# Sigmoid attention and a SwiGLU block on one core: exchanged PSUM tiles, visits one product later, a split transfer, two sums moved

## The chip, the cores and the metric

The kernel runs on one core of one Trainium2 chip. The metric is the time of the program on the device, in microseconds. Before the change it is 401.79 us, the median of three runs (401.12 to 402.68). The profiled execution took 401.11 us, of which its page shows a span of 399.1 us.

## The reference

```python
# q, k, v: (8, 12, 448, 64); 8 batches, 12 heads, 448 positions
scores = (q @ k.transpose(0, 1, 3, 2)) / sqrt(64) - log(448)
attn   = 1 / (1 + exp(-scores))             # sigmoid, no softmax over the row
x      = (attn @ v).transpose(0, 2, 1, 3).reshape(3584, 768)
g      = x @ w_gate                         # (768, 1536)
val    = x @ w_val                          # (768, 1536)
out    = (g * sigmoid(g) * val) @ w_out     # (1536, 768)
```

Since the sigmoid needs no sum over a row, every chunk of scores can be finished by itself. The inputs are float32; the kernel computes scores in bf16 and the rest in float16 with float32 sums.

## The kernel before

**Tiling.** The heads of a batch are taken in three groups of four, called quads here; quad n belongs to batch n // 3, so there are 24. The keys of a quad are cut into C = 7 chunks of 64 positions. One chunk of scores for four heads is four products of 64x64 tiles that fill both banks of one PSUM tile (`qk_tile`, L246-261). One ScalarE instruction makes the sigmoid of both banks (`sig_tile`, L273), or two, one for each bank, where the tile is wanted back early (L270). When seven chunks of a quad are through, `pv` (L276-314) multiplies them with V in 28 products and copies the two banks to two tiles xT on VectorE (L304 and L312). If `flip(n)` holds, the scores of the second pair of heads are written to the other half of the partitions, V is loaded by two transfers of 112 KB with heads in that order (L195), and the second xT tile is filled by one copy of 128 partitions. Otherwise V is one transfer of 224 KB (L197) and that copy is two of 64 partitions.

**The FFN.** Batches go in pairs pb = 0 to 3. `ffn1(b, f)` makes one block of 128 hidden features of one batch: six products for the gate and six for the value (L324), a sigmoid on ScalarE (L347), and two VectorE instructions (L349, L353) that leave the block hT. For the last two pairs most blocks are made two at a time by `double` (L434-507), which uses seven half-size products in place of eight, with sums of inputs made ahead; it is called the fast pair below. The output product of a pair is made likewise, in `ffn2_group` (L595), from sums of hT that `make_sums` (L533) computes on VectorE (L554). A group g is a generator that goes through seven products, in the order 1, 2, 6, 5, 7, 3, 4, with a snapshot or an addition out of PSUM after each (L644 on ScalarE, L646 and L651 on VectorE). `ffn2_part(pb, moves)` says which group steps next: (0, 1, 0, 1) does two products each of groups 0 and 1, and (0,) * 5 the rest of group 0.

**PSUM.** All of it is a ring of four tiles of two banks. `Banked` hands them out in turn, and a tile that an output group holds is left out (`kept`). When a group ends, the turn is set behind its tile. A product that writes a tile waits until the last reader of that tile is done.

**The order of work** on TensorE is the order in which the program is written out; nothing reorders it at run time. A planner in Python (L947-968) lists the FFN units with durations it assumes, and puts a visit to the attention in between when its due time has passed: a visit is four chunks (0 to 3) or three (4 to 6) of a quad. `attn_step` (L785-793) carries it out: two score tiles, then `pv` of the quad before if it is complete, then the other one or two. A condition in L953 keeps visits from some places, for instance right after a part of an output stage that mixes two groups. `budget` says how many of the pending sums VectorE makes after a unit, and the sums left over are made later.

**Other queues.** GpSimd casts q and k to bf16 (L204), issues the loads of V and of the weights, and makes some sums of its own, among them those of the rows left over at the end of each batch (`rest_sums`, L593). After each three-chunk visit of quad n it waits for the last sigmoid (`behind_visit`, L855), casts quad n+2 and issues its V; SyncE then transposes the casts by DMA (L211), loads q and k of quad n+4 (L183), and stores outputs (L565). Each queue goes in order.

Of the kernel before, what the change touches and what calls it, by code (L numbers as in the profile page):

```python
# [20 lines left out]
def kernel(  # L21
# [17 lines left out]
    NJ = H // 4  # L39
    NP = H // 2  # L40
    NF = DFF // 128
    NQ = B * NJ
    W2 = 2 * S
    LAST = B // 2 - 1
# [29 lines left out]
    ring_at = [0]  # L74
    ring_user = [None] * 4
    kept = set()
# [107 lines left out]
        qkv_st[(n, which)] = st  # L184

    def flip(n):
        return n > 5

    def load_v(n):
        t = v16p.tile([128, 2, S], FP16, tag="v16", name=f"v16_{n}")  # L190
# [55 lines left out]
    def qk_tile(n, c, at=None):  # L246
        sd = Banked(at=at)
        sc = sd.t
        qt, kt = qT[(n, 0)], qT[(n, 1, c)]
        for w in range(2):  # L250
            for h2 in range(2):
                r = slice(h2 * 64, h2 * 64 + 64)
                g = (w ^ (h2 and flip(n))) * 64
                nc.tensor.matmul(  # L254
                    out=sc[g:g + 64, h2, :S],
                    lhsT=kt[r, w * 64:(w + 1) * 64],
                    rhs=qt[r, :, w * 64:(w + 1) * 64],
                    start=True,
                    stop=True,
                )  # L260
        return sd
# [54 lines left out]
    V, G = nc.vector, nc.gpsimd  # L316
# [59 lines left out]
    def fast_w(i, kind):  # L376

        s, lo, hi = gcut[i]
        cs = slice(lo * 128, hi * 128)
        b11, b21 = wg16[s][:, 0::2, cs], wg16[s][:, 1::2, cs]  # L380
        b12, b22 = wv16[s][:, 0::2, cs], wv16[s][:, 1::2, cs]
        n = JT * (hi - lo) * 128
        at = {3: 0, 2: 1, 4: 2}.get(kind)
        if kind == 1:
            t = b12
        else:
            if i == 0:
                t = half_of(stg_a)[:, at * n:(at + 1) * n]
            elif i == 1 and kind == 3:
                t = half_of(ramp_a)[:, 8 * FW * hw:8 * FW * hw + n]  # L390
            elif i == 1:
                t = pt_f[:, (at - 1) * n:at * n]
            elif i == 2:
                t = pt_f[:, (at + 2) * n:(at + 3) * n]
            elif i == 3:
                o = JT * FW * 128 * 5 + NF * 128
                t = pt_f[:, o + at * n:o + (at + 1) * n]
            else:
                t = osp.tile([128, DM], FP32, tag="osb", name=f"g{kind}").bitcast(FP16)[:, :n]
            t = t.rearrange("p (j n) -> p j n", j=JT)  # L400
        gT[(i, kind)] = t
        a, b, op = {
            3: (b22, b12, SUB), 1: (b12, b11, SUB), 2: (b22, gT.get((i, 1)), SUB), 4: (b21, gT.get((i, 2)), SUB),
        }[kind]
        V.tensor_tensor(out=t, in0=a, in1=b, op=op)
# [118 lines left out]
    budget = {}  # L524
# [42 lines left out]
    def rest_h(pb, i):  # L567
        if pb == LAST:
            a, at = pt_f, 5 * JT * FW * 128
        else:  # L570
            a, at = half_of(ramp_a), 8 * FW * hw
        return a[:, at + i * 128:at + (i + 1) * 128]

    def rest_s(pb, kind, i):
        if pb == LAST:
            at = ((kind - 1) * HF + i) * 128
            return half_of(stg_a)[:, at:at + 128]
        return hS[(pb, kind, i)][:, :128]

    def keep_rest(pb, fs, copy):  # L580
        for f in fs:
            copy(out=rest_h(pb, f), in_=hT[(pb - 1, f)].rearrange("p b s -> p (b s)")[:, (C - 1) * 128:])

    def rest_sums(pb, eng):
        of = lambda f: hT[(pb, f)].rearrange("p b s -> p (b s)")[:, (C - 1) * 128:]
        for kind in (1, 2, 3, 4):
            for i in range(HF):
                f = 2 * i
                a, b, op = {
                    1: (of(f), of(f + 1), ADD), 2: (rest_s(pb, 1, i), rest_h(pb, f), SUB),  # L590
                    3: (rest_h(pb, f), of(f), SUB), 4: (rest_h(pb, f + 1), rest_s(pb, 2, i), SUB),
                }[kind]
                yield eng.tensor_tensor(out=rest_s(pb, kind, i), in0=a, in1=b, op=op)  # L593
# [124 lines left out]
    for pb in range(B // 2):  # L718
        for b in (2 * pb, 2 * pb + 1):
            f1_start[b] = tt  # L720
            for f in range(NF):
                if f not in FAST.get(pb, ()):
                    if b or f > 2:
                        units.append((FU1, ffn1, (b, f)))
                    tt += FU1
            f1_end[b] = tt
        for f in FAST.get(pb, ())[::2]:
            extra = {
                (LAST - 1, 0): ((0, 4), (1, 2)), (LAST - 1, 2): ((1, 4), (2, 3)),
                (LAST - 1, 4): ((2, 1), (2, 2)), (LAST - 1, 6): ((2, 4), (3, 3), (3, 1), (3, 2)),  # L730
                (LAST - 1, 8): ((3, 4),),
                (LAST, 0): ((4, 3),), (LAST, 2): ((4, 1),), (LAST, 4): ((4, 2),), (LAST, 6): ((4, 4),),
            }.get((pb, f), ())
            units.append((FU4, double, (pb, (f, f + 1), [lambda a=a: fast_w(*a) for a in extra])))
            tt += FU4
        skip = lambda: None
        w = lambda *a: lambda: [w_sum(*b) for b in a]
        o_units = [(0.0, make_sums, (99,))]
        part = lambda moves, *a: o_units.append((FU3 * len(moves) / 7, ffn2_part, (pb, moves) + a))
        if pb == 0:  # L740
            fill[(1, 7)] = [lambda: w_sum(0, 3), lambda: w_sum(0, 2)]
            fill[(1, 9)] = [lambda: w_sum(0, 1)]
            o_units += [(0.0, w_sum, a) for a in ((1, 3), (1, 2))]
            part((0, 1, 0, 1), ("1654", "154"), (skip, skip, w((1, 1))))
            part((0,) * 5, "", (w((0, 4), (1, 4)),))
            copies = [lambda f=f: keep_rest(1, (f, f + 1, f + 2), V.tensor_copy) for f in range(0, NF, 3)]
            part((1,) * 5, "", copies)
            part((2,) * 7, "654")
        elif pb == 1:
            part((0, 1, 0, 1), "1")  # L750
            part((0,) * 5)
            part((1,) * 5, "", (lambda: list(rest_sums(1, G)),))
            part((2,) * 3)
            part((2,) * 4)
            part((3,) * 3, "", (skip, lambda: fast_w(1, 3), lambda: fast_w(1, 1)))
            part((3,) * 4)
            o_units.append((0.0, sums_of_x, (LAST - 1,)))
        else:
            part((0, 1) * 7, "1", (skip, lambda: keep_rest(LAST, range(NF), nc.scalar.copy)) if pb < LAST else ())
            if pb == LAST:  # L760
                part((3,) * 7)
            part((2,) * 7)
        units += o_units
        tt += sum(u[0] for u in o_units)


    FIRST = f1_end[0] - 5.0
    PACE = ((2 * NJ, FIRST + 3.5), (3 * NJ - 1, FIRST + 28.9), (3 * NJ - 0.5, f1_end[1] - 0.1), (3 * NJ, FIRST + 40.5), (3 * NJ + 2, FIRST + 55.6), (6 * NJ + 1, f1_end[B - 5] - 1.0), (6 * NJ + 1.5, f1_end[B - 5]), (NQ, f1_end[B - 5] + 1.0))
    tiles = [(n, c) for n in range(NJ, NQ) for c in range(C)]
    visits = [tiles[:2], tiles[2:4]]  # L770
# [3 lines left out]
    vtime = []  # L774
    for grp in visits:
        n, c = grp[0]
# [3 lines left out]
        else:  # L780
            at = n + (0.5 if c else 0.0)
# [3 lines left out]
    def attn_step(group, pvs):  # L785
        late = 1 if pvs else 0
        for part in (group[:2], group[2:]):
            scs = [(n, c, qk_tile(n, c)) for n, c in part]
            while pvs:
                pv(pvs.pop(0))  # L790
            for i, (n, c, sc) in enumerate(scs):

                sig_tile(n, c, sc, split=len(group) == 4 and part[0] == group[0] and i == late)
# [12 lines left out]
    for i in range(8):  # L806
# [8 lines left out]
    copies = [  # L815
        trans_part(Dq, 0, 0, 0, 0, QS, V, dq[:, :QS]),
        trans_part(Dq, 1, 0, 0, QS, C, V, dq[:, QS:]),
    ]
# [130 lines left out]
    tcur = 3 * FU1  # L949
    since, was_v = 99.0, 9  # L950
    was, was_args = ffn1, (0, 2)
    for dur, fn, args in units:
        if visits and tcur >= vtime[0] and not (was is ffn2_part and len(set(was_args[1])) > 1) and not (was is ffn1 and was_args[0] < 2 and was_args[1] == 0) and (vtime[0] < FIRST + 4 or since > (3.8 if len(visits[0]) > 3 and visits[0][0][0] < 4 * NJ else 2.0)):  # L953
            seq.append((None, visits.pop(0), 0 if fn is ffn1 else 1))
            vtime.pop(0)
            since, was_v = 0.0, 0
        seq.append((fn, args, not visits and was_v == 1))
        was, was_args = fn, args
        was_v += dur > 0.0
        since += dur  # L960
        tcur += dur

    for i, (fn, args, _) in enumerate(seq):
        if fn is ffn1:
            ahead = [len(a) if f is None else 0 for f, a, _ in seq[i + 1:i + 3]] + [0, 0]
            budget[args] = 0 if args == (3, NF - 1) else 3 if ahead[0] else 0 if ahead[1] == 4 else 2
        if fn is double:
            args[2].append(lambda: make_sums(5))

# [70 lines left out]
```

## Time and profile before

| | before |
|---|---|
| Time, median of three | 401.79 us |
| TensorE busy | 388.6 us, 97% of the span |
| VectorE busy | 251.4 us, 63% |
| ScalarE busy | 237.3 us, 59% |
| GpSimd busy | 123.3 us, 31% |
| First FFN products | about 22 us after the start |
| First output stage (pair 0) | 98.1 to 124 us |
| Second output stage (pair 1) | 207.5 to 244 us |
| First fast pair | from 259.1 us |

The page names an instruction by its line in the kernel, its engine, and the tiles it writes and reads. In the timeline a line gives the start, the time from the first to the last of the instructions merged in it, and in brackets how long the engine had been idle before it and what ended that. A matmul's time there (0.35 us for 448 columns) is that of one instruction from end to end; since they overlap, the pace is read from one start to the next.

### The profile page before, as it was taken

The page shows a single profiled execution, that of the slowest core. Times are in us where ns is not written, and L with a number is a line of the kernel's source. Part 1 is how long each engine was busy: PE and PEld are TensorE (multiplying, and loading weights), DVE is VectorE, ACT ScalarE, POOL GpSimd, SP SyncE. Part 2 cuts the span into 40 slices and gives each one's busy share as a digit, 9 for nine tenths or more (in the row PEclk, how much of TensorE's full clock was granted, in tenths as well). Part 3 has the DMA queues.
Part 4 walks back from the last instruction along what each step waited for, and adds up shares of the span by engine and source line. Part 5 has one row for each costly group of instructions (what it writes and reads, how often), then busy time and mean ns, then how long its engine had stood idle before and what let it go on. Part 6 is the DMA issues. An engine that isn't in the chain of part 4 may idle for free.

```text
span 399.1 us, 8113 instructions
## 1 busy us (share of the span) xinstructions
PE 388.6 (97%) x3110; PEld 201.9 (51%) x3110; DVE 251.4 (63%) x505; ACT 237.3 (59%) x385; POOL 123.3 (31%) x203
## 2 busy tenths in 40 slices
PE   7799999999999999999999999999999999999995
PEld 3444544445555444444455555455555655555653
DVE  2637646688643444466674564699986558787553
ACT  5966785746456797779773467966653055656000
POOL 4538041421311353343330958600007400000900
PEclk9999999999999999999999999999999999999999
DMA  8999979996599777797778878000000520000055
GB/s 273 246 246 256 241 166 261 183 169 98 143 279 232 173 163 163 163 186 163 163 164 192 198 161 201 3 2 1 1 2 0 159 79 2 2 2 0 2 169 147
DMA packets 65574, 54.39 MB, mean 136 GB/s; under 512 B 36032, under 2 KB 61728, under 8 KB 65536
## 3 DMA queue, kind: packets, MB, share of 16 engines
q1 hardware_dynamic: 49264, 37.04, 35.1%
q0 software_dynamic: 15360, 15.34, 24.3%
q10 hardware_dynamic: 912, 1.51, 1.2%
q8 instruction: 24, 0.39, 0.4%
q14 instruction: 14, 0.11, 0.1%
HBM read 47.19 MB, written 11.01 MB: 146 GB/s over the span
## 4 chain that ended last, share of the span: by engine, by line
PE 93%; DMA 3%; DVE 1%; ACT 1%; issue 0%; SPq 0%; POOL 0%; DVEq 0%; ACTq 0%
PE ps_D L324 31%; PE ps_D L633 24%; PE ps_D L460 22%; PE ps_D L254 8%; PE ps_D L289 8%; DMA v<-in_v_dram 2%; DMA st<-in_q_dram 1%; DVE xT L312 1%; PE ps_D L223 0%; DVE xT L304 0%; ACT osb L644 0%; DVE T L229 0%; ACT small L490 0%; DVE osb L646 0%; DVE stg_a L646 0%
## 5 line engine op out<-in xcount | busy, mean ns | idle before, releaser
L273 ACT ACTIVATE pt_a<-ps_D 128x896 f16<-128x896 f32 x148 | 127.1, 920 | 41.5 <-PE ps_D L254 39.8
L324 PE MATMUL ps_D<-xT,wg 128*128 128x448 f16 x312 | 69.2, 353 | 0.2
L324 PE MATMUL ps_D<-xT,wv 128*128 128x448 f16 x312 | 68.5, 353 | 0.0
L349 DVE TENSOR_TENSOR t<-ps_D,s 128x448 f16<-128x448 f32 x52 | 32.4, 624 | 54.8 <-ACT s L347 54.2
L470 ACT ACTIVATE snap<-ps_D 128x448 f32<-128x448 f32 x66 | 34.2, 542 | 29.4 <-PE ps_D L460 27.5
L254 PE MATMUL ps_D<-T,T 64*64 64x448 bf16 x644 | 44.6, 358 | 2.2 <-DVE T L229 1.2
L324 PEld LDWEIGHTS <-wg 128*128 128x128 f16 x312 | 27.8, 98 | 34.0 <-issue 12.1
L324 PEld LDWEIGHTS <-wv 128*128 128x128 f16 x312 | 30.4, 98 | 28.9 <-issue 0.6
L347 ACT ACTIVATE s<-ps_D 128x448 f16<-128x448 f32 x52 | 28.7, 551 | 22.8 <-PE ps_D L324 22.8
L204 POOL CAST c<-stg_a 128x896 bf16<-128x896 f32 x40 | 36.5, 939 | 14.5 <-DMA stg_a<-in_q_dram 10.3
L633 PEld LDWEIGHTS <-S 128*128 128x128 f16 x312 | 30.2, 98 | 20.9 <-issue 1.3
L633 PE MATMUL ps_D<-ramp_a,S 128*128 128x384 f16 x234 | 40.2, 326 | 0.0
L289 PE MATMUL ps_D<-pt_a,v 64*64 64x448 f16 x672 | 36.0, 350 | 0.5 <-DMA v<-in_v_dram 0.5
L353 DVE SCALAR_TENSOR_TENSOR hT<-ps_D,t 128x448 f16<-128x448 f32 x52 | 32.5, 625 | 5.4
L651 DVE SCALAR_TENSOR_TENSOR osb<-ps_D,osb 128x384 f32<-128x384 f32 x40 | 22.3, 557 | 19.0 <-PE ps_D L633 16.7
L855 POOL CAST held<-S 128x1 bf16<-128x1 f16 x3 | 0.6, 190 | 107.7 <-ACT osb L644 55.7
L646 DVE TENSOR_SCALAR osb<-ps_D 128x384 f32<-128x384 f32 x37 | 20.6, 557 | 18.1 <-PE ps_D L633 15.1
L633 PEld LDWEIGHTS <-hT 128*128 128x128 f16 x228 | 22.1, 98 | 15.6 <-issue 1.3
L855 POOL CAST held<-pt_a 128x1 bf16<-128x1 f16 x13 | 2.5, 190 | 87.3 <-ACT pt_a L273 87.3
L460 PE MATMUL ps_D<-xS,wv 128*128 128x448 f16 x132 | 28.6, 352 | 0.1
L254 PEld LDWEIGHTS <-T 64*64 64x64 bf16 x644 | 15.2, 105 | 25.3 <-issue 17.7
L460 PE MATMUL ps_D<-xT,wg 128*128 128x448 f16 x132 | 26.8, 353 | 0.0
(109 smaller groups left out, 497.4 us busy)
## 6 DMA issues: line engine op xcount, KB each, us to landing
out_dram<-osb SPq DMA_DIRECT2D x45, 192.0 KB, 4.0
stg_a<-in_q_dram SPq DMA_DIRECT2D x18, 448.0 KB, 5.5
stg_a<-in_k_dram SPq DMA_DIRECT2D x18, 448.0 KB, 6.5
v<-in_v_dram POOLq DMA_DIRECT2D x36, 112.0 KB, 4.4
wg<-in_moe_w_gate_dram POOLq DMA_DIRECT2D x4, 576.0 KB, 11.8
wv<-in_moe_w_val_dram POOLq DMA_DIRECT2D x4, 576.0 KB, 13.4
wo<-in_moe_w_out_dram POOLq DMA_DIRECT2D x4, 576.0 KB, 8.7
v<-in_v_dram POOLq DMA_DIRECT2D x6, 224.0 KB, 10.8
```

The lines of the kernel that those rows point to most:

```text
L204: eng.tensor_copy(out=t.rearrange("p c h d -> p h c d"), in_=st.rearrange("p h (c d) -> p h c d", c=C))
L254: nc.tensor.matmul(out=sc[g:g + 64, h2, :S], lhsT=kt[r, w * 64:(w + 1) * 64], rhs=qt[r, :, w * 64:(w + 1) * 64], start=True, stop=True,)
L273: nc.scalar.activation(out=pt, in_=sc[:, :, :S], func=SIGM, bias=sbias, scale=qkscale)
L289: nc.tensor.matmul(out=P[g:g + 64, h2, :S], lhsT=vt[r, h2, c * D:(c + 1) * D], rhs=pt[r, h2, :], start=(c == 0), stop=(c == C - 1),)
L324: nc.tensor.matmul(out=D.t[:, i, :S], lhsT=(wg16, wv16)[i][f // FW][:, pr, cs], rhs=xT[(b, pr)], start=(pr == 0), stop=(pr == NP - 1),),
L347: D.read(nc.scalar.activation(out=s16, in_=D.t[:, 0, :S], func=SIGM), 0)
L349: D.read(nc.vector.tensor_tensor(out=t1, in0=D.t[:, 0, :S], in1=s16, op=MULT), 0)
L353: nc.vector.scalar_tensor_tensor(out=hT[(b // 2, f)][:, b % 2, :], in0=D.t[:, 1, :S], scalar=hsc(b // 2), in1=t1, op0=MULT, op1=MULT),
L460: nc.tensor.matmul(out=D.t[:, bank, :S], lhsT=W(f, j), rhs=X(j), start=(start and j == 0), stop=(stop and j == JT - 1), skip_group_check=True,
L470: D.read(nc.scalar.mul(out=o, in_=D.t[:, bank, :S], mul=scale), bank)
L633: nc.tensor.matmul(out=D.t[:, bank, :hw], lhsT=l, rhs=B_(i), start=(first and i == order[0]), stop=(i == order[-1]), skip_group_check=True,),
L651: D.read(nc.vector.scalar_tensor_tensor(out=o, in0=i, scalar=1.0 / hsc(pb), in1=o, op0=MULT, op1=ADD), bank)
```

## The change

There are four edits. The first is in `attn_step`: in a visit of four chunks with a value product in it, and with no tile held, the third chunk takes the tile after the next in the ring, which is the first chunk's, and the fourth takes the next, which was the FFN unit's before the visit. It is for the third chunk to wait on another reader. The second keeps visits from the place right behind the rest of group 0 in an output stage, and cuts the rest of group 1 in one product and four, so that a visit can come behind that one product. The third lets `flip` hold for quad 5 too, so its V comes in two transfers and its second xT by one copy. The fourth sets the budget after the last single block of the third pair to 0, so that the two sums made there are made within the first fast pair.

```diff
     def flip(n):
-        return n > 5
+        return n > 4
...
             copies = [lambda f=f: keep_rest(1, (f, f + 1, f + 2), V.tensor_copy) for f in range(0, NF, 3)]
-            part((1,) * 5, "", copies)
+            part((1,), "", copies[:1])
+            part((1,) * 4, "", copies[1:])
...
-            part((1,) * 5, "", (lambda: list(rest_sums(1, G)),))
+            part((1,), "", (lambda: list(rest_sums(1, G)),))
+            part((1,) * 4)
...
     def attn_step(group, pvs):
         late = 1 if pvs else 0
         for part in (group[:2], group[2:]):
-            scs = [(n, c, qk_tile(n, c)) for n, c in part]
+            if late and part != group[:2] and len(part) == 2 and not kept:
+                a = ring_at[0] % 4
+                scs = [(n, c, qk_tile(n, c, at=(a + i) % 4)) for (n, c), i in zip(part, (1, 0))]
+                ring_at[0] += 2
+            else:
+                scs = [(n, c, qk_tile(n, c)) for n, c in part]
...
-        if visits and tcur >= vtime[0] and not (was is ffn2_part and len(set(was_args[1])) > 1) and ...
+        if visits and tcur >= vtime[0] and not (was is ffn2_part and (len(set(was_args[1])) > 1 or was_args[1] == (0,) * 5)) and ...
...
-            budget[args] = 0 if args == (3, NF - 1) else 3 if ahead[0] else 0 if ahead[1] == 4 else 2
+            budget[args] = 0 if args in ((3, NF - 1), (2 * LAST - 1, NF - 1)) else 3 if ahead[0] else 0 if ahead[1] == 4 else 2
```

More of the change, by code (lines that the diff above doesn't have):

```diff
@@ L952 @@
     for dur, fn, args in units:
-        if visits and tcur >= vtime[0] and not (was is ffn2_part and len(set(was_args[1])) > 1) and not (was is ffn1 and was_args[0] < 2 and was_args[1] == 0) and (vtime[0] < FIRST + 4 or since > (3.8 if len(visits[0]) > 3 and visits[0][0][0] < 4 * NJ else 2.0)):
+        if visits and tcur >= vtime[0] and not (was is ffn2_part and (len(set(was_args[1])) > 1 or was_args[1] == (0,) * 5)) and not (was is ffn1 and was_args[0] < 2 and was_args[1] == 0) and (vtime[0] < FIRST + 4 or since > (3.8 if len(visits[0]) > 3 and visits[0][0][0] < 4 * NJ else 2.0)):
             seq.append((None, visits.pop(0), 0 if fn is ffn1 else 1))
```

## The prediction

> **What bounds the kernel now.** I read the engine busy line and the chain that ended last first. Both say TensorE:
>
> ```profile
> PE 388.6 (97%) x3110; PEld 201.9 (51%) x3110; DVE 251.4 (63%) x505; ACT 237.3 (59%) x385; POOL 123.3 (31%) x203
> ...
> PE 93%; DMA 3%; DVE 1%; ACT 1%; issue 0%; SPq 0%; POOL 0%; DVEq 0%; ACTq 0%
> ```
>
> No other engine comes near, so an edit pays only where it closes a pause of TensorE. The waits of TensorE by line sum to few microseconds, and the largest lie in the first 21 us, which the change barely touches. So I went through the timeline and asked of each run of matmuls how long it should last. A 448-column matmul follows the last one after 0.189 us (12 at L324 from 142.13 to 144.51, less the switch below), a 384-column one after 0.1625, and four 64x64 products run together in 0.189. What is left over is the switch between the 128x128 and 64x64 shapes, 0.10 to 0.13 us each way, and pauses at five kinds of place.
>
> (a) A visit of four chunks; timeline of quad 12's:
>
> ```profile
> 140.22 0.62 DVE L349 TENSOR_TENSOR t<-ps_D,s 128x448 f16<-128x448 f32 x1 [2.29 <-ACT s L347]
> 140.25 1.49 PE L289 MATMUL ps_D<-pt_a,v 64*64 64x448 f16 x28
> 140.29 0.92 ACT L273 ACTIVATE pt_a<-ps_D 128x896 f16<-128x896 f32 x1
> 140.95 0.62 DVE L353 SCALAR_TENSOR_TENSOR hT<-ps_D,t 128x448 f16<-128x448 f32 x1
> 141.63 0.57 PE L254 MATMUL ps_D<-T,T 64*64 64x448 bf16 x8
> ```
>
> The 28 products of L289 end at 140.25 + 28/4 x 0.189 = 141.58. The third chunk starts at 141.63, just after hT ends at 141.57: it reuses the PSUM tile of the FFN unit before the visit. The first chunk's sigmoid was over at 141.21.
>
> (b) Inside output stages:
>
> ```profile
> 107.03 0.49 ACT L644 ACTIVATE osb<-ps_D 128x384 f32<-128x384 f32 x1 [2.43 <-PE ps_D L633]
> 107.57 1.52 PE L289 MATMUL ps_D<-pt_a,v 64*64 64x448 f16 x28
> ...
> 216.36 1.10 PE L254 MATMUL ps_D<-T,T 64*64 64x448 bf16 x12
> 216.47 0.56 DVE L646 TENSOR_SCALAR osb<-ps_D 128x384 f32<-128x384 f32 x1 [0.42 <-PE ps_D L633]
> ```
>
> Each visit needs the tile that group 0 just finished, and waits for its last snapshot.
>
> (c) After quad 5's value product:
>
> ```profile
> 64.01 1.26 DVE L312 CAST xT<-ps_D 64x448 f16<-64x448 f32 x2
> 64.94 0.72 PE L324 MATMUL ps_D<-xT,wg 128*128 128x448 f16 x2
> 65.50 0.73 PE L324 MATMUL ps_D<-xT,wv 128*128 128x448 f16 x3
> ```
>
> The second matmul of the pair needs the xT that the two half copies fill until 65.27.
>
> (d) First fast pair:
>
> ```profile
> 259.43 0.36 DVE L554 TENSOR_TENSOR S<-hT,hT 128x384 f16<-128x384 f16 x1
> 259.82 0.36 DVE L554 TENSOR_TENSOR S<-S,hT 128x384 f16<-128x384 f16 x1
> 262.53 1.08 ACT L470 ACTIVATE snap<-ps_D 128x448 f32<-128x448 f32 x2 [1.52 <-DVE small L483]
> 263.67 1.30 PE L460 MATMUL ps_D<-xS,stg_a 128*128 128x448 f16 x6
> 265.02 1.29 PE L460 MATMUL ps_D<-xS,wv 128*128 128x448 f16 x6
> ```
>
> Six matmuls from 263.67 end at 264.81; the next start at 265.02, behind an ACT chain that DVE held up.
>
> [...] with 0.10 to 0.13 us per change; I count that as a fixed price of a visit. [...] Here 224 KB took 10.8 us and 112 KB 4.4 us at the median, but most of the large ones fell in the crowded first 40 us, so I take no gain or loss in bandwidth from the split.
>
> **The change, part by part.**
>
> *Exchanged tiles.* The third chunk takes the first chunk's tile, the fourth that of the FFN unit. The third now waits for the first sigmoid, over 0.37 us before it is needed in (a) and 0.31 or more in every later such visit. The fourth needs hT 0.19 us later than the third did, and hT ended at the third's due time or up to 0.05 after. Both waits vanish. In seven visits (before 53.2, 141.6, 159.4, 169.4, 187.0, 197.0, 207.0) the pause is 0.05 us, and the switch that follows is 0.025 longer than in an unpaused visit (0.127 for 0.102): 0.077 each, 0.54. At 251.7 it is 0.10 + 0.025. Sum 0.67. One is eaten: quad 13's transposed keys land at 147.61, when its first product starts (147.65). So 0.59. Further on, the second tile of the next three-chunk visit waits for the fourth sigmoid instead of the third: that ends at 143.84, the tile is needed at 144.70.
>
> *Visits one product later.* Working the planner's loop through with its constants, two visits move, quad 9's first and quad 19's second; each is now behind group 1's third product (6 matmuls, 0.975 us). The snapshots ending at 107.52 and 217.03 are then long done. At 106.92 eight products took 0.649 us where 0.403 is usual (0.25); at 216.36 twelve took 1.034 for 0.694 (0.34). Sum 0.59. The number of switches stays.
>
> This adds an order on GpSimd. In the second output stage the 24 sums of line 593 (222.52 to 231.8, 9.3 us) were queued behind the visit's casts; now they stand ahead of them:
>
> ```profile
> 219.47 0.19 POOL L855 CAST held<-pt_a 128x1 bf16<-128x1 f16 x1 [11.18 <-ACT pt_a L273]
> 219.59 1.82 POOL L204 CAST c<-stg_a 128x896 bf16<-128x896 f32 x2
> 220.55 2.58 SPq L211 DMA_TRANSPOSE T<-c  x2
> 222.52 2.34 POOL L593 TENSOR_TENSOR S<-hT,hT 128x128 f16<-128x128 f16 x6
> ```
>
> Behind them wait quad 21's casts, its V, its transposes, and on the SP queue two loads and group 1's stores. The first of the sums overwrite columns that group 0's fourth product reads last, from 212.4 to 213.4. GpSimd is idle from 208.3, so they can run from about 212.7 to 222.0; the casts start 2.5 us later than at 219.59. The second transpose, issued at 221.89, took 6.7 us to land (longest in this stretch): 228.6, and is first used at 232.31. Of 3.7 us slack, 2.5 + 0.3 goes and 0.9 remains. Cost 0. If the sums waited for group 1's third product (217.4), they would end at 226.7, casts 7 us late, and TensorE would wait 3.6 us.
>
> *Quad 5's V.* One full copy (0.61) replaces two half copies (1.26): xT is ready at 64.6, needed at 65.12. The 0.18 us pause goes. Cost: two GpSimd issues of 0.59 for one of 0.70 at 34.04, so wg and wv of the fourth weight block are issued 0.5 us later. In the trace such issues wait for the landing of the one eight earlier (20.58 behind a landing at 20.02), and with one more in the row the second half of quad 6's V waits for wv's landing at 42.3, 2 us. Behind it on GpSimd are casts whose data lands at 51, and that V is used after 76. The fourth block landed by 49.4 and is used at 53.7. Cost 0.
>
> *Two sums.* The two L554 rows in (d), 0.67 us of DVE, move behind the first pair's additions. The ACT snapshot that waited for DVE starts up to 0.5 us earlier, so product 3 starts unpaused: 0.2. In the pair DVE then makes four sums instead of two (0.6 more, less 0.67 earlier), so v at 265.00 keeps its time and product 4 at 265.95 finds its tile read at 265.6.
>
> Sum: 0.59 + 0.59 + 0.18 + 0.2 = 1.56; 401.79 - 1.6 = **400.2 us**, or -0.4%.
>
> **Rivals.** *Half comes*: a freed wait uncovers the next (transposes as at 147.65, an ACT whose sigmoids leave 0.67 us idle per visit). For it: hT was late because ACT was; against it: slack of 0.3 us or more at nearly all other places. -0.8: 401.0. *More comes*: earlier visits ease ACT and DVE beyond the places I counted (0.21 us at 114.2, 0.10 at 127.5), and the profiled run before, 401.11, says that the median of three lies high by up to 0.7. -2.3 to -2.5: 399.4. *Slower*: quad 21's transposes come late, 3.6 us, against the 1.6: 401.79 + 2.0 = 403.8. For it: 9.3 us of sums stand ahead of a transfer with 3.7 us slack. Against it: before, group 1's products ran at 218 to 222 while the sums of the same buffers came at 222.5 and later, so order is kept by columns, not by whole buffers.
>
> **How the numbers follow.** Forecast 0.62, more 0.20, half 0.10, slower 0.08. -0.5% is 399.8, and medians of three that spread by 1.5 us move by some 0.5: a third of the forecast's weight crosses it. Faster 0.20 + 0.20 = 0.40; same 0.42 + 0.10 = 0.52; slower 0.08. The range, leaving out the slower case and the tails: 399.0 to 401.5.
>
> **What would show it.** L289 followed by L254 after exactly 1.324 us in all visits; no pause in the visits near 108 and 217; the sums of line 593 from about 212 and quad 21's transposes issued near 222 with TensorE unbroken at 231; one L312 copy at 64; product 3 of the first pair 1.14 us after product 7. A TensorE wait on T near 231, or a new wait on ACT ahead of the third chunks, would make it wrong.

## The result, and the profile after

The changed kernel takes **399.69 us** (median of six runs, 399.61 to 399.92), the kernel before, in the same comparison, 401.20 (six runs, 401.08 to 402.68). The ratio is 0.9955, with a 95% interval of 0.9941 to 0.9970: 1.5 us less. The prediction was 400.2 us, 1.6 less than 401.79; the range of 399.0 to 401.5 holds the result. A later comparison of the same two kernels gave 399.97 and 401.46, ratio 0.9966 [0.9955, 0.9978].

The page after, engine line and chain of waits:

```profile
PE 386.3 (97%) x3110; PEld 201.5 (51%) x3110; DVE 250.9 (63%) x504; ACT 237.5 (60%) x385; POOL 124.6 (31%) x204
...
PE 94%; DMA 3%; DVE 1%; ACT 0%; issue 0%; SPq 0%; POOL 0%; DVEq 0%; ACTq 0%
```

The number of matmuls is the same, 3110, and TensorE still sets the end. Its busy time fell by 2.3 us although its work did not change. A matmul's record lasts 0.35 us and the next one starts 0.19 us later, so a record covers most of a short pause: in the kernel before, four products start at 216.58 and the next four at 217.08, 0.50 us apart for 0.19, and only 0.15 us of it shows as idle. So the totals can't say where the 1.5 us came from. The starts of TensorE's matmuls can, when each run of matmuls is held against its pace.

Quad 12's visit, in the timeline after:

```profile
140.13 0.62 DVE L349 TENSOR_TENSOR t<-ps_D,s 128x448 f16<-128x448 f32 x1 [2.27 <-ACT s L347]
140.17 1.49 PE L289 MATMUL ps_D<-pt_a,v 64*64 64x448 f16 x28
140.86 0.62 DVE L353 SCALAR_TENSOR_TENSOR hT<-ps_D,t 128x448 f16<-128x448 f32 x1
141.49 0.55 PE L254 MATMUL ps_D<-T,T 64*64 64x448 bf16 x8
```

L254 follows L289 after 1.32 us, where it was 1.38. The block hT still ends at 141.48, on the due time of the third chunk to 0.01 us, but the third chunk no longer asks for it: it writes the tile of the first chunk. The late reader was not made faster, it was taken out of the way.

The two visits inside output stages, in the timeline after:

```profile
107.21 0.49 ACT L644 ACTIVATE osb<-ps_D 128x384 f32<-128x384 f32 x1 [2.43 <-PE ps_D L633]
108.08 0.57 PE L254 MATMUL ps_D<-T,T 64*64 64x448 bf16 x8
108.48 1.49 PE L289 MATMUL ps_D<-pt_a,v 64*64 64x448 f16 x28
...
215.85 0.56 DVE L646 TENSOR_SCALAR osb<-ps_D 128x384 f32<-128x384 f32 x1 [0.42 <-PE ps_D L633]
216.72 0.76 PE L254 MATMUL ps_D<-T,T 64*64 64x448 bf16 x12
217.41 2.12 PE L633 MATMUL ps_D<-ramp_a,S 128*128 128x384 f16 x12
```

Each snapshot (107.70, 216.41) is over before the visit begins at 108.08 and 216.72, and the products take 0.40 and 0.69 us from start to start instead of 0.65 and 1.03.

Quad 5's second copy and the first fast pair:

```profile
64.25 0.61 DVE L312 CAST xT<-ps_D 128x448 f16<-128x448 f32 x1
64.74 0.73 PE L324 MATMUL ps_D<-xT,wv 128*128 128x448 f16 x3
65.31 0.54 PE L324 MATMUL ps_D<-xT,wg 128*128 128x448 f16 x2
...
261.08 1.11 ACT L470 ACTIVATE snap<-ps_D 128x448 f32<-128x448 f32 x2 [1.16 <-PE ps_D L460]
262.58 1.30 PE L460 MATMUL ps_D<-xS,stg_a 128*128 128x448 f16 x6
263.72 1.30 PE L460 MATMUL ps_D<-xS,wv 128*128 128x448 f16 x6
264.86 1.30 PE L460 MATMUL ps_D<-xT,stg_a 128*128 128x448 f16 x6
```

There is one copy at L312 where there were two, done at 64.86 and wanted at about 65.3. In the pair the products now follow at 1.14 us throughout; before, 263.67 to 265.02 was 1.35.

From here on, a kernel's **steady part** is the stretch from TensorE's first unbroken FFN units (26.45 us in the profile before, 26.89 after) to the end of its last fast-pair product (367.21 before, 365.92 after). It is 1.73 us shorter after. What lies ahead of it, the front, moves from profile to profile by more than the change is worth (26.3 to 28.2 us in the profiles of this study): TensorE waits there for loads, for instance quad 0's V, which landed at 12.87 in the one and 13.44 in the other, and nothing of the change is issued before 34 us. In the two profiles with the latest fronts (28.24 with the sums put back, 27.86 with the weights first, both below) the granted clock is part of it: it was 0.50 for 3.41 us from 13.2, and quad 0's value products took 2.6 us up to the next products, for 1.35 in the changed kernel. Here they are in the profile with the weights first and in that of the changed kernel:

```profile
13.19 2.79 PE L289 MATMUL ps_D<-pt_a,v 64*64 64x448 f16 x28 [0.72 <-DMA v<-in_v_dram]
...
13.48 1.52 PE L289 MATMUL ps_D<-pt_a,v 64*64 64x448 f16 x28 [1.16 <-DMA v<-in_v_dram]
```

In two more profiles it was 0.50 for 3.41 us from 8.2 and 8.7 (edit three taken back, and the two sums alone), with fronts of 26.82 and 26.69. Why the clock fell near 13 in the one pair and not in the rest isn't shown: TensorE was busy for 2.0 and 2.1 of the 3.4 us before, for 1.6 to 2.4 in profiles where it did not fall. So times say how much the change is worth, and the steady part says where.

### The profile page after: what moved, and what is told of

Its sections match the earlier page's. It is cut to its first block, busy times and chain, and to the rows that moved or that the text cites. A ratio compares the mean times of both kernels' runs of the same rounds, so it can differ in the third digit from the quotient of the medians.

```text
span 397.9 us, 8117 instructions
## 1 busy us (share of the span) xinstructions
PE 386.3 (97%) x3110; PEld 201.5 (51%) x3110; DVE 250.9 (63%) x504; ACT 237.5 (60%) x385; POOL 124.6 (31%) x204
## 4 chain that ended last, share of the span: by engine, by line
PE 94%; DMA 3%; DVE 1%; ACT 0%; issue 0%; SPq 0%; POOL 0%; DVEq 0%; ACTq 0%
PE ps_D L324 31%; PE ps_D L633 24%; PE ps_D L460 22%; PE ps_D L254 8%; PE ps_D L289 8%; DMA v<-in_v_dram 2%; DMA st<-in_q_dram 1%; PE ps_D L223 0%; DVE xT L304 0%; DVE xT L312 0%; DVE T L229 0%; ACT pt_a L273 0%; DVE stg_a L646 0%; ACT pt_a L270 0%; SPq L166 0%
## 5 line engine op out<-in xcount | busy, mean ns | idle before, releaser
L254 PE MATMUL ps_D<-T,T 64*64 64x448 bf16 x644 | 44.0, 356 | 2.0 <-DVE T L229 1.0
L633 PEld LDWEIGHTS <-S 128*128 128x128 f16 x312 | 30.2, 98 | 21.1 <-issue 1.4
L633 PE MATMUL ps_D<-ramp_a,S 128*128 128x384 f16 x234 | 40.5, 326 | 0.0
L289 PE MATMUL ps_D<-pt_a,v 64*64 64x448 f16 x672 | 35.9, 349 | 1.2 <-DMA v<-in_v_dram 1.2
L646 DVE TENSOR_SCALAR osb<-ps_D 128x384 f32<-128x384 f32 x37 | 20.6, 557 | 19.1 <-PE ps_D L633 16.2
L633 PEld LDWEIGHTS <-hT 128*128 128x128 f16 x228 | 22.1, 98 | 15.6 <-issue 1.2
L254 PEld LDWEIGHTS <-T 64*64 64x64 bf16 x644 | 15.4, 105 | 24.1 <-issue 17.0
```

The source lines that it names most:

```text
L254: nc.tensor.matmul(out=sc[g:g + 64, h2, :S], lhsT=kt[r, w * 64:(w + 1) * 64], rhs=qt[r, :, w * 64:(w + 1) * 64], start=True, stop=True,)
L289: nc.tensor.matmul(out=P[g:g + 64, h2, :S], lhsT=vt[r, h2, c * D:(c + 1) * D], rhs=pt[r, h2, :], start=(c == 0), stop=(c == C - 1),)
L633: nc.tensor.matmul(out=D.t[:, bank, :hw], lhsT=l, rhs=B_(i), start=(first and i == order[0]), stop=(i == order[-1]), skip_group_check=True,),
```

## The experiments

### Each edit alone

Four kernels, each the kernel before with one edit. Exchange alone:

```diff
-            scs = [(n, c, qk_tile(n, c)) for n, c in part]
+            if late and part != group[:2] and len(part) == 2 and not kept:
+                ... # third chunk takes the first chunk's tile
```

> The kernel before with the exchange of PSUM tiles alone. Theory (each edit closes pauses of TensorE that it names, and they add): the 28 value products are followed by the third chunk after 1.324 us in every visit, eight pauses go, 7 x 0.077 + 0.126 = 0.67 us, of which 0.08 may be eaten by transposes near 147.6; time 0.6 to 0.7 us under before. The pauses near 64, 107, 216 and 265 us stay. Rival (the freed wait uncovers the next one): half of it, 0.3 us, with new gaps ahead of the fourth chunk or of the unit behind the visit.

The visits alone:

```diff
-            part((1,) * 5, "", copies)
+            part((1,), "", copies[:1])
+            part((1,) * 4, "", copies[1:])
...
-        ... not (was is ffn2_part and len(set(was_args[1])) > 1) ...
+        ... not (was is ffn2_part and (len(set(was_args[1])) > 1 or was_args[1] == (0,) * 5)) ...
```

> The kernel before with the visits in output stages one product later, alone. Theory: the pauses near 107 (0.25 us, and 0.03 more at the switch behind it) and near 216 (0.34 us) go, the others stay; 0.6 us under before. Rival (GpSimd's sums now ahead of quad 21's casts cost something): TensorE waits for T near 231 us, and the gain is under 0.3 us or a loss.

Quad 5's V in two transfers alone:

```diff
-        return n > 5
+        return n > 4
```

> The kernel before with the flip of quad 5 alone: V in two transfers, second xT in one copy. Theory: the 0.18 us pause near 65 us goes and nothing else moves; 0.2 us under before. Rival (the split costs time in the crowded first 40 us, which would explain why TensorE stood 0.44 us later at 26 us in the changed kernel's profile): TensorE's first full unit again starts about 0.4 us later, and the time is 0.0 to 0.3 us over before.

The two sums alone:

```diff
-            budget[args] = 0 if args == (3, NF - 1) else ...
+            budget[args] = 0 if args in ((3, NF - 1), (2 * LAST - 1, NF - 1)) else ...
```

> The kernel before with the two sums moved into the first fast pair, alone. Theory: the 0.21 us pause ahead of the pair's sixth product (third of the seven by number, near 265 us) goes; 0.2 us under before. Rival (the four sums then made in the pair delay VectorE's reading of the PSUM tile ahead of product 4): the pause moves to product 4, and the time is that of before.

Measured, all four against 67 runs of the kernel before (401.47 us):

| alone | us | ratio | steady part |
|---|---|---|---|
| exchange | 400.76 | 0.9985 [0.9978, 0.9991] | -0.74 |
| visits | 401.00 | 0.9990 [0.9983, 0.9998] | -0.54 |
| V of quad 5 | 401.47 | 0.9999 [0.9990, 1.0008] | -0.15 |
| two sums | 401.14 | 0.9994 [0.9987, 1.0001] | -0.21 |
| sum of the four | | -0.32% | -1.64 |
| all together | 399.69, 399.97 | 0.9955, 0.9966 | -1.73 |

The first two are resolved by time, the last two are not: their intervals hold 1. Block by block the profiles show what closed: with the exchange alone the 0.077 us of seven visits, 0.126 of the eighth, and 0.07 ahead of quad 13's visit; with the visits alone the pauses at 106.92 (0.25) and 216.36 (0.34) and 0.03 at the switch behind the first, while 0.07 was added ahead of quad 13's; with quad 5's V alone 0.18 at 64, less 0.04 ahead of quad 13's; with the sums alone 0.21 in the first pair. There the keys of quad 13 came in time, which took 0.07 away ahead of its visit, and the third chunk of that visit then waited, which gave 0.08 back: the tile's wait had been hidden behind the keys'. That a next wait takes the place of the closed one is wrong within 0.1 us in all four. The edits add, as far as the blocks show: without quad 13's visit and the block ahead of it the four sum to 1.65 us, and all together give 1.66.

The changed kernel with edit three taken back shows the same edit from the other side.

```diff
-        return n > 4
+        return n > 5
```

> The changed kernel without the flip of quad 5. Theory: the pause of 0.18 us near 65 us is back and nothing else, 0.2 us over the changed kernel, 1.3 under before. Rival (the split of V costs 0.3 us in the first 25 us): 0.1 to 0.2 us under the changed kernel.

It took 399.68 us (ratio 0.9955 [0.9939, 0.9971]), as the changed kernel does; its profile shows the pause near 65 back: the two products at 65.24 take 0.56 us up to the next start, for 0.38 in the changed kernel. That was expected to be the only difference, but there is another: 0.16 us came ahead of quad 13's visit, where its keys landed at 147.65 and the first product started at 147.69. That quad 5's edit is worth 0.18 us rests on the profiles alone.

### The changed kernel again

> The changed kernel once more, beside the next three on one chip. Theory: 1.5 us under before; from TensorE's first full unit to its last pause 1.73 us shorter than before, with the difference made by when the first loads land (TensorE's first full unit between 26.3 and 26.9 us).

399.97 us (five runs, 399.79 to 400.32). The steady part equals that of the first profile to 0.01 us, block by block.

### What the order on GpSimd costs

In the prediction the rival on the slower side was GpSimd's new order in the second output stage. First, the sums put back behind the visit:

```diff
-            part((1,), "", (lambda: list(rest_sums(1, G)),))
-            part((1,) * 4)
+            part((1,))
+            part((1,) * 4, "", (lambda: list(rest_sums(1, G)),))
```

> The changed kernel with GpSimd's 24 left-over sums put back behind quad 19's visit, as before. Theory (the new order on GpSimd had slack): quad 21's transposes are issued some 3 us earlier, TensorE's pauses stay those of the changed kernel, time within 0.2 us of it. Rival (the new order costs part of what the visit gives): 0.2 us or more under the changed kernel.

400.34 us, ratio 0.9974 [0.9964, 0.9983] against 0.9966 [0.9955, 0.9978] for the changed kernel in the same comparison: not told apart by time. The profiled run is the slowest of the twelve, 401.79. It has one new pause, 0.34 us ahead of quad 22's visit, and 0.21 ahead of quad 13's. GpSimd's timeline and then TensorE's, of this kernel:

```profile
224.44 2.35 POOL L593 TENSOR_TENSOR S<-hT,hT 128x128 f16<-128x128 f16 x6
...
233.79 1.80 POOL L204 CAST c<-stg_a 128x896 bf16<-128x896 f32 x2
...
242.38 2.58 SPq L211 DMA_TRANSPOSE T<-c  x2
243.18 0.57 PE L254 MATMUL ps_D<-T,T 64*64 64x448 bf16 x8 [0.27 <-DMA T<-c]
```

The sums from 224.44 hold back the next quad's casts to 233.79, and so its transposes: the second was issued at 236.10, landed at 243.14, and quad 22's visit was due at 242.84. Counted from the front (28.24 in this profile), the sums stand where they stood before, since the visit they follow now comes a product later; but quad 22's visit is due 1.2 us earlier than before (214.6 for 215.8 us after the front). The transposes had 2.6 us to spare in the kernel before (landed 239.62, used 242.25, after a flight of 5.44); here 1.2 of it went to the earlier visit and 1.6 to a flight of 7.04. In the changed kernel the same keys landed at 237.64 and were first used at 241.29. So both theories missed: GpSimd's new order, which I had booked as a risk that costs nothing, keeps slack for quad 22 that the old order would not have at the new pace. How often that slack would run out, one profile does not say: with the flight of 5.44 there would have been 1.3 us left.

GpSimd's timeline of the changed kernel:

```profile
212.16 2.35 POOL L593 TENSOR_TENSOR S<-hT,hT 128x128 f16<-128x128 f16 x6 [4.43 <-PE ps_D L633]
...
219.09 2.36 POOL L593 TENSOR_TENSOR S<-ramp_a,S 128x128 f16<-128x128 f16 x6
221.38 0.20 POOL L862 CAST held<-pt_a 128x1 bf16<-128x1 f16 x1
221.50 1.83 POOL L204 CAST c<-stg_a 128x896 bf16<-128x896 f32 x2
```

The sums begin at 212.16, within group 0's fourth product (211.76 to 212.73), half a microsecond before the 212.7 predicted, and hold quad 21's casts until 221.50. The transposes are issued at 222.48 and 224.37, landed at 227.15 and 228.94, and are first used at 231.35: 2.4 us of slack. To see that slack end, the sums were made twice; the values are the same.

```diff
-            part((1,), "", (lambda: list(rest_sums(1, G)),))
+            part((1,), "", (lambda: list(rest_sums(1, G)) + list(rest_sums(1, G)),))
```

> The changed kernel with GpSimd's 24 left-over sums made twice over (the second time with the same values), so that 9.2 us more stand ahead of quad 21's casts. Theory (that order is harmless only up to the slack of quad 21's transposes, 2.4 us in the changed kernel's trace: landed 228.9, used 231.35): TensorE waits 9.2 - 2.4 = 6.8 us for T near 231 us, time 6.5 to 8 us over the changed kernel. Rival (the transposes have other slack, or GpSimd's sums don't hold them up): under 3 us over.

408.62 us (two runs), ratio 1.0178 [1.0151, 1.0205]. The waits of TensorE, and windows of 7 and 1 us (length, then the busy time of PE, PEld, DVE, ACT and POOL, the granted clock of TensorE, the DMA share and GB/s):

```profile
PE ps_D L254 <- DMA T<-c: 6.8, 1, 6.8
...
219.00:226.00 7.00, 7.00 (x75) 3.85 (x72) 3.95 (x7) 3.62 (x6) 7.00 (x20) 1.00 0.04 14
...
231.00:238.00 7.00, 0.23 (x4) 0.19 (x8) 0.52 (x1) 0.00 (x0) 5.28 (x9) 0.86 0.81 143
...
239.00:240.00 1.00, 1.00 (x16) 0.43 (x12) 0.00 (x0) 1.00 (x3) 0.00 (x0) 0.50 1.13 283
...
243.00:244.00 1.00, 1.00 (x8) 0.59 (x6) 0.37 (x1) 0.55 (x1) 0.00 (x0) 1.00 1.37 100
```

The pause is 6.84 us for the 6.8 expected, 9.2 of added sums less 2.4 of slack. TensorE took none of the work that follows the visit into the pause: from 231 to 238 it was busy for 0.23 us. But the time rose by 8.9 us over 399.7, and the steady part by 9.4. The rest is the clock: it was 0.50 for 6.83 us, from 235.97, some 5.0 us into the pause, to 242.80. So the first 5.0 us of work behind the pause ran at 0.50, and the visit's blocks and the one behind took 2.4 us longer than in the changed kernel. The long wait cost a third more than its length. The pauses that the change closes, 0.05 to 0.34 us, cost only themselves: the clock reads 1.00 around them (in the profile before, from 26 to 399 us throughout).

### What is left at 114 us

In the changed kernel the longest pause left in the steady part is 0.21 us in a visit at 114.10. I took it for a snapshot on ScalarE that stands ahead of the visit's sigmoids, and moved that one to VectorE:

```diff
-            part((0, 1, 0, 1), ("1654", "154"), (skip, skip, w((1, 1))))
+            part((0, 1, 0, 1), ("1654", "15"), (skip, skip, w((1, 1))))
```

> The changed kernel with group 1's last snapshot in the first output stage on VectorE instead of ScalarE. Theory: the 0.21 us pause left near 114.5 us comes from ScalarE doing that snapshot ahead of the visit's first sigmoid; with it gone 0.1 to 0.2 us under the changed kernel. Rival (the fourth chunk waits for the snapshot on whichever engine): the pause stays within 0.05 us, time unchanged.

399.80 us, the pause unchanged at 0.21 over a switch. The timeline of this kernel:

```profile
113.99 1.10 PE L254 MATMUL ps_D<-T,T 64*64 64x448 bf16 x16
114.10 0.56 DVE L646 TENSOR_SCALAR osb<-ps_D 128x384 f32<-128x384 f32 x1
114.48 0.98 ACT L270 ACTIVATE pt_a<-ps_D 128x448 f16<-128x448 f32 x2 [2.82 <-PE ps_D L254]
115.08 2.11 PE L633 MATMUL ps_D<-wo,hT 128*128 128x384 f16 x12
```

The snapshot is now at L646, and the first sigmoid still starts 0.49 us after the products (0.50 in the changed kernel, behind the snapshot at L644). ACT had been idle for 2.82 us: it was never late. L633 starts at 115.08, just when the first half of the sigmoid ends (115.03). That the next output product waits for the tile of the visit's first chunk is read from these times; the number of the rival was right, its reason was not this one.

### When the same edit is not free: quad 4

If a split transfer costs nothing, quad 4's should cost nothing either.

```diff
-        return n > 4
+        return n > 3
```

> The changed kernel with quad 4's V in two transfers as well. Theory (a split in the crowded first 40 us costs nothing): pauses after 27 us as in the changed kernel, time within 0.2 us of it. Rival (each split delays the first loads by 0.3 us): TensorE's first full unit at 27.2 us, time 0.3 us over the changed kernel.

400.59 us (21 runs), ratio 0.9979 [0.9973, 0.9986]: 0.6 above the 399.97 of the same comparison. Timeline of this kernel:

```profile
30.19 0.84 POOL L138 DMA_DIRECT2D wg<-in_moe_w_gate_dram  x1 [2.33 <-DMA wv<-in_moe_w_val_dram]
...
41.56 1.30 PE L324 MATMUL ps_D<-xT,wg 128*128 128x448 f16 x6
43.20 1.31 PE L324 MATMUL ps_D<-xT,wv 128*128 128x448 f16 x6 [0.34 <-DMA wv<-in_moe_w_val_dram]
```

In the traces of the kernel before and of the changed one, no DMA that GpSimd issues starts before the one eight earlier has landed, and five and six of them start 0.28 to 0.55 us behind that landing. With one more in the row, the third block of the gate's weights is issued at 30.19, behind a landing at 29.91, and not at 26.73, behind one at 26.45, as in the changed kernel. The value weights behind it land at 43.15 and not at 42.61, and TensorE starts with them at 43.20. In the changed kernel it starts at 42.97, so these weights have 0.36 us to spare. Quad 5's split doesn't draw on that: its V is issued behind them, at 34.39 for 33.58, and without the split the slack is much the same (0.27 in the kernel before, 0.35 in the changed one with edit three taken back). What stands behind quad 5's V is the fourth block of weights, whose value half landed at 49.64 and was first used at 55.20. The front was not late (26.62), so the rival, which put the loss there, was wrong too. Then the same with that block of weights issued first:

```diff
+    w_load("g", 2)
     load_v(4)
-    w_load("g", 2)
```

> The changed kernel with V of quad 4 in two transfers as well, and the third block of the gate's weights issued ahead of V of quad 4 rather than behind it. Theory: what e8_v4 lost at the front was only the late issue of that weight block (30.19 instead of 27.26 us), which moved the landing of the value weights to 43.15. With the block issued first, the value weights land at about 42.4 again and the pause of 0.5 us ahead of TensorE's value products near 42 is gone; the time is within 0.2 us of the changed kernel, 399.5 to 400.0. Rival: the second transfer of quad 4 itself takes the bandwidth or the place in the queue of eight, whatever the order: the pause of 0.3 to 0.5 us near 42 stays, and the time is 400.2 to 400.8, as in e8_v4.

The value weights land at 42.31, as the theory had it, and TensorE waits for nothing there: the landing moved with the order of the row, by 0.84 us. The missing pause by itself proves less, because the front of this profile is late (27.86): TensorE comes to these products at 43.94, when weights that land at 43.15 would have been in time too. With the changed kernel's 42.97, 42.31 is in time and 43.15 is not. But the time is 400.58 us (20 runs), ratio 0.9974 [0.9965, 0.9984], where the rival put it. Both kernels with quad 4 split show two further pauses that the changed kernel has not, 0.25 us near 121, where VectorE waits for an output store to land (2.8 us with quad 4 split, 2.4 in the changed kernel, where it holds nothing up), and 0.18 near 290. In this profile they are all that is left, since its steady part is 0.42 longer than the changed kernel's. The one before, 1.05 longer, also has the 0.50 at 42 and 0.12 ahead of quad 13's visit. Why they come with quad 4's split, and how much of the medians is a late front (this profile is of a run of 401.32, with the slow clock near 13; the fastest runs of the two, 399.92 and 399.82, are near the changed kernel's 399.61), stays open.

## Why the prediction was right, point by point

**The account of TensorE's pauses held.** Predicted and measured, from the blocks of the two profiles: exchange 0.59, measured 0.67 and 0.07 more ahead of quad 13's visit; visits 0.59, measured 0.59 and 0.03 at a switch; quad 5's V 0.18 and 0.18; two sums 0.2 and 0.21. The sum is 1.56 against 1.73 in the steady part and 1.5 (0.9955) in time. The prediction speaks of five kinds of place and lists four, (a) to (d); the four hold all of it.

**The term that was off in the exchange** is the 0.08 taken off for quad 13's transposed keys. In the profile after, the first product there waited for nothing. But it isn't a steady number: ahead of that visit the profiles show anything from 0 to 0.21 us over the switch, with the landing of its second transpose. That took 4.2 to 4.8 us in the six profiles without a pause and 4.9 to 5.3 in the seven with one. It should have been a spread of 0.2 us in the range, not a fixed loss.

**The level was 0.5 too high**, not the gain: the forecast started from 401.79, the median of three runs, and the wider comparisons gave 401.20 to 401.47 for the same kernel. The prediction named this under the rival with more gain (up to 0.7 too high) and did not take it into the number. With 401.3 as the start it would have been 399.7.

**Quad 21's slack** was 2.4 us and not 0.9. The term that failed is the 6.7 us of a transpose, taken as the longest in the stretch: it took 4.6. That alone would have left 3.0; the other 0.6 went because the second transpose was issued 2.87 us after the first cast began, where the kernel before had 2.30. The doubled sums show it from the other side, 9.2 - 6.84 = 2.4. The rival that made the kernel 2 us slower asked for sums that wait for group 1's third product; they began at 212.16, before it. The order of reads by columns that was put against this rival fits: they start while group 0's fourth product, which reads those buffers, still runs (to 212.73).

**The half and the fuller rival.** No freed wait uncovered another: each edit alone gave its blocks in full. Nor did the visits ease anything farther off: the pauses at 114 and 127 are there after, 0.21 and 0.10 us.

**Quad 5's split at cost 0** held, and the wait of 2 us that it puts on the second half of quad 6's V is there, 1.83 us. It held because of the place in the row: what is issued behind it had slack, 5.6 us at the value half of the fourth block. One V earlier the same edit stands ahead of weights with 0.3 to 0.4 us to spare, and loses 0.5.

**The price of a switch** between the 64x64 and 128x128 shapes, 0.10 to 0.13 us, stays in all kernels; it was right to count none of it as a gain, except the 0.025 that a switch behind a pause is longer. That part went with the pauses, 0.025 in each of eight visits.

## What to carry to other kernels

Where one engine is busy for 97% of the span, hold each run of its instructions against its own pace: the excess of each block over its count times its step gave four kinds of pauses, and what closing them brings, to 0.2 us in a sum of 1.7. A pause on a reused buffer can be closed by handing out the buffers in another order (0.67 us here); the reader need not become faster. And whether an edit costs nothing in a queue depends on what stands behind it there, so write down how much slack that has: here it was 2.4 us behind the sums, 5.6 at the weights behind quad 5's split, and 0.36 at those behind quad 4's.

## What the runs showed of the hardware that was not expected

A pause of 6.84 us of TensorE cost 8.9 us in time and 9.4 in the steady part, because the clock granted was 0.50 for the first 5.0 us of work after it. Around the changed kernel's 1.16 us ahead of quad 0's value products it read 1.00, as around the pauses of 0.05 to 0.34 us. In two profiles it was 0.50 for 3.41 us from 13.2 with no such long pause just ahead: TensorE had been busy for 2.0 and 2.1 of the 3.4 us before. The flight of one and the same transpose (L211, second of a pair, in the second output stage) differs from profile to profile: quad 21's took 6.7 us in the kernel before and 4.6 in the changed one, quad 22's 5.4 in both and 7.0 with the sums put back. A slack below about 2 us behind it may run out in some runs, by an estimate from these differences.
